# Attention and routed experts in one kernel: a new order of all operations, with the products on zeros at other places

## The chip, the cores and the metric

One core of a Trainium2 chip runs the whole program. The metric is device time in microseconds (us); of the kernel before there are three timed runs and one profiled execution. TensorE (PE, with its weight load PEld) multiplies matrices into PSUM; VectorE (DVE), ScalarE (ACT) and GpSimd (POOL) compute element by element; GpSimd and SyncE (SP) issue the DMAs. Every engine works through its own instruction stream in order, and waits on semaphores for the others.

## What is computed

A sliding-window attention (8 batches, 8 heads, 576 positions, width 64, window 32 to either side) feeds a mixture of 8 experts, of which the token's modality and its logits choose one:

```python
scores = scale * np.matmul(q, k.transpose(0, 1, 3, 2))
mask = np.abs(pos[:, None] - pos[None, :]) <= window
scores = np.where(mask, scores, -1000000000.0)
attn = np.exp(scores - np.max(scores, axis=-1, keepdims=True))
attn = attn / (np.sum(attn, axis=-1, keepdims=True) + 1e-09)
x = np.matmul(attn, v)              # then [8 * 576, 512]
logits = x @ w_gate + modality_bias[modality_id]
e_idx = np.argmax(logits, axis=1)
gate_w = softmax(logits)[np.arange(N), e_idx]
h = np.maximum(x[mask] @ w1[e], 0.0)            # mask: e_idx == e
out[mask] = gate_w[mask, None] * (h @ w2[e])
```

There are 4608 tokens and two modalities. For such inputs two experts are used in fact, one for each modality; the kernel loads these two, sorts the tokens by modality while it gathers them, checks at its end that the choice holds, and has a slow general path that is not taken here.

## The kernel before

The program is a list of 867 operations, the string `ORDER` (line 34 on). A token such as `SB3.1:4567` names an operation, its indices, and after the colon the PSUM banks (of eight) that it writes; `/v`, `/a` and `/p` choose VectorE, ScalarE or GpSimd where an operation may run on more than one. One loop (line 1022 on, the last lines of the kernel's own part) calls the operations in the list's order, and each appends its instructions to the stream of its engine. Semaphores are set by the data and the banks that operations share. So the list alone decides what stands behind what on each engine, and which bank has to be read out before it is written again.

The operations, by name:

- `l` (L213) and `lv` (L229) load query, key (index 1 in the middle: key; 0: query) and values from GpSimd's queue; `W` (L643, L645) loads the two experts' weights, each 1 MB; `Km`, `Ki`, `Kg` are small loads on SP, `Ki` that of the modality ids into a tile which `Kh` clears first (L311).
- `t` (L653) transposes query or key of one half of a batch on VectorE, 1.25 us each. `MA`, `MB` write the first batch's mask by products (L662, L666).
- `SA`, `SB` (L685) are the products of the scores in two parts, each into four banks; `sa`, `sb` (L693, L696) their exponentials on ScalarE; `M` (L710) multiplies with the window mask on VectorE, from batch 1 on. `Kb` builds that mask (L425 on ScalarE, L427 on VectorE). `Kp`, `Kq`, `Ko`, `Kw` fill padding and constants.
- `V` (L727) multiplies with the values, 18 products for a pair of heads; `v` (L739, L740) normalises.
- `s0` to `s19` turn the ids into places: a cast (L165), a transpose by a product (L461), then counts, ranks and offsets. `G`, `Jo`, `Je` build one-hots on VectorE and GpSimd, `Jm` (L535) the list of output rows.
- `X` (L761) gathers the tokens by products with one-hots; `pa`, `pb` (L781, L795) copy them to their sorted places on ScalarE.
- `U` (L899) is the first expert product, eight instructions of 256 columns for a group, `u` (L914, L916) its rectifier; `D` (L925) the second, four instructions of 512 columns for a half, `y` (L935, L937) the scaling with the gate; `O` (L944) writes 128 rows by an indirect DMA. `L` (L826), `lo`, `E`, `sm`, `rc` are the routing.
- `c` are the checks at the end; `c13` casts three flags (L165), `c14` sums them by one product (L1004).
- `n4.256:1` issues four products of a zero tile with itself, 256 columns each, into bank 1 (L953): they compute nothing that is read. There are 64 of them.

Batches follow one another in this pipeline: while the expert products of the first tokens run, scores of later batches stand between them.

Of the kernel before, what the change touches and what calls it, by code (L numbers as in the profile page):

```python
# [34 lines left out]
Km Kw0/v n4.256:0 l0.1.0/p l0.0.0/p n4.256:0 Kp0/a Kj/p n4.256:0 l0.1.1/p e0/v e1/v n4.256:0 Kp1/v Kn0/p Kq1/v n4.256:0  # L35
Kq0/v l0.0.1/p Ke/v n4.256:0 Kw2/v l1.0.2/p Kh/v t0.0.1/v Ki n4.256:0 Kw1/p Kn1/p MA0.0:0123 e2/v e3/v n4.256:4 e4/v
t0.0.0/v n2.256:4 Kg n2.256:4 n2.256:4 lv0.0/p n2.256:4 Ko1/v n2.256:4 t0.1.1/v n2.256:4 n2.256:4 SA0.0 Kc5/p MA0.1:4567
sa0.0/a t0.1.0/v Kc1/p Kv/p lv0.1/p SA0.1 MB0.0:0123 Kc3/p sa0.1/a t1.1.0/v SB0.0 l1.1.2/p s0/a W1.0/p Ko0/v t1.0.0/v
MB0.1:4567 sb0.0/a Kc2/p SB0.1 Kc0/p n2.256:0 s1:0 sb0.1/a V0:12 Kc4/p s2/v s3/v s4 s5 n2.256:3 v0/v n2.256:3 lv1.0/p
n2.256:3 s6/v Kb/a s8/v V2:34 s11/v e6/v s12/p V1:12 e7/p v2/v Kc6/p s7 V3:56 n2.256:7 v1/v W1.1/p n2.256:3 s9/a s10/a  # L40
n2.256:4 r0/a n2.256:0 n2.256:0 t1.0.1/v lv1.1/p r1/a v3/v SA1.0:0123 W2.0/p s13/v sa1.0/a t1.1.1/v SB1.0:4567 l2.0.2/p
s15/v Ko2/v sb1.0/a e8/v SB1.1:0123 s14/v s17/v G0/v s16/v c0/v Je1.0/v Je0.0/v sb1.1/a X0.0:5 Jy2/v M5/v Je0.1/p X0.4:4
X0.1:7 l2.1.2/p Jy10/v Jo1/v Je0.2/p pb0.0/a X0.2:2 pa0.0/a l3.1.2/p M4/v V5:01 pb0.1/a pa0.1/a e5/p l3.0.2/p pb0.2/a
X0.3:5 pa0.2/a v5/v V4:67 Je1.1/p pb0.3/a pa0.3/a Je1.2/p Jo0/v pb0.4/a SA1.1:0123 lv2.0/p pa0.4/a v4/v Jm0:5 sa1.1/a
U0.1:4 G1/v Kc7/p Jo2/v U0.0:6 u0.1/a Je2.0/v U1.3:0 M7/v Je2.1/p U1.0:7 Je3.0/v u1.3/a W2.1/p M6/v u0.0/a V7:12 e9/p
u1.0/a U0.2:6 Je3.1/v Je2.2/v v7/v lv2.1/p V6:34 u0.2/a U0.3:0 r2/a v6/v Je3.2/p U1.2:1 u0.3/a Jo3/v L0:7 X1.2:0 X1.0:6
lo0/v Jx0/v Jm1:3 pa1.0/a X1.1:7 D0.1.0:4 Je5.0/v pb1.0/a Jx1/v Jo5/v Je5.1/p pb1.1/a D0.0.0:6 E0/a pa1.1/a sm0/v
Je4.0/v pb1.2/a rc0/v G2/v Je4.1/p X1.3:3 pa1.2/a X1.4:7 D0.0.1 pa1.3/a t2.0.0/v pa1.4/a D0.1.1 pb1.3/a Jo4/v pb1.4/a
U2.3:0 y0.1/a Je5.2/v Je4.2/v t2.0.1/v L1:3 u1.2/a Jm2:7 y0.0/a U3.2:5 lo1/v u2.3/a s19/v Jo6/v SB2.0:1234 Je7.0/v
U2.2:0 Je7.1/v sb2.0/a Je7.2/v Jx2/v U2.1:6 t2.1.1/v U2.0:7 t2.1.0/v u2.1/a u2.2/a SA2.0:1234 Jo7/v u2.0/a U3.3:6 E1/a  # L50
sa2.0/a Je6.0/v U3.1:7 t3.0.1/v Je6.1/p U1.1:0 Je6.2/p u3.1/a M9/v l4.0.2/p u3.3/a SA2.1:1234 u1.1/a M8/v lv3.0/p
D2.0.0:7 sa2.1/a Jm3:0 D2.0.1 l4.1.2/p Jx3/v sm1/v u3.2/a Jy1/v lv3.1/p Jy3/v SB2.1:0123 Jy0/v Jy4/v t3.0.0/v D2.1.0:6
sb2.1/a Jy5/v V9:45 rc1/v D2.1.1 v9/v y2.0/a V8:01 M10/v y2.1/a SB3.0:2345 U3.0:6 v8/v sb3.0/a D1.1.0:7 M11/v V10:01
r3/a Jy8/v Jy6/v V11:45 v10/v D1.1.1 u3.0/a v11/v D1.0.0:0 y1.1/a Jy7/v X2.0:2 Jy9/v X2.1:3 G3/v X2.2:7 O0.1/p pa2.0/a
D3.1.0:1 pb2.0/a t4.1.0/v pa2.1/a X2.3:6 pb2.1/a O0.0/p D3.0.0:2 pa2.2/a t4.0.0/v pb2.2/a D1.0.1 pa2.3/a pb2.3/a X2.4:7
D3.0.1 y1.0/v pb2.4/a pa2.4/a t3.1.1/v O1.0/p D3.1.1 SA3.0:4567 t3.1.0/v O2.0/p U5.0:0 sa3.0/a t4.1.1/v U4.2:3 y3.0/v
# [1170 lines left out]
```

## Time and profile before

| | |
|---|---|
| three timed runs, median (lowest to highest) | 212.38 us (212.2 to 212.52) |
| profiled execution, its own time | 213.69 us |
| its span, first to last instruction | 212.0 us |
| busy in the span: PE, PEld, DVE, ACT, POOL | 193.3, 140.2, 151.8, 133.5, 99.3 us |
| mean granted clock of TensorE | 0.970 of full speed |
| products on zeros | 64, first at 1.3, last at 21.2 us |

The busy times are shares of one span in which the stages have different limits, so they say little alone; the stretches below split the span. A wait is named by the engine and line that ended it ("<-PE banks L685"); "issue" is time for which the profile shows no reason, and "remote" a release by nothing that the profile shows. The granted clock is 1.00 at 2.4 GHz and 0.50 at 1.2 GHz. Matmuls are pipelined and their ends are modelled.

### The profile page before, as it was taken

How to read it: one execution, taken by the hardware profiler on the slowest of the kernel's cores; microseconds unless marked ns; L12 is line 12 of the kernel's file. 1: busy time of each engine (PE TensorE's matmuls, PEld its weight loads, DVE VectorE, ACT ScalarE, POOL GpSimd, SP SyncE). 2: the span in 40 equal slices, each digit the busy share in tenths (PEclk: the TensorE clock that was granted, in tenths of full speed). 3: DMA queues.
4: the chain of work that ended last, by engine and by line, in shares of the span. 5: the costliest groups of instructions: out<-in, count | busy, mean ns of one | idle time of the engine just before them, and what ended most of it. 6: DMA issues, size and time to landing. Idle time of an engine off the chain costs nothing.

```text
span 212.0 us, 6172 instructions
## 1 busy us (share of the span) xinstructions
PE 193.3 (91%) x2538; PEld 140.2 (66%) x2561; DVE 151.8 (72%) x300; ACT 133.5 (63%) x224; POOL 99.3 (47%) x138
## 2 busy tenths in 40 slices
PE   7869489999999989999999999999999999999940
PEld 5647278768675577668765885686597668566510
DVE  3868999799889978899899569887376527311610
ACT  5268696498896466896796879759975622244110
POOL 7887699730803483368650853330160322025350
PEclk9999859999999999999999999999999999999995
DMA  4999999999999459999999899225030121113212
GB/s 73 175 174 201 194 208 194 213 212 193 196 190 192 172 129 211 194 178 173 220 190 72 268 165 128 99 102 201 0 148 6 54 99 53 49 49 149 101 56 56
DMA packets 47629, 30.41 MB, mean 143 GB/s; under 512 B 38851, under 2 KB 38891, under 8 KB 47339
## 3 DMA queue, kind: packets, MB, share of 16 engines
q0 software_dynamic: 46576, 27.79, 83.1%
q1 hardware_dynamic: 1019, 2.16, 3.0%
q8 instruction: 22, 0.36, 0.7%
q14 instruction: 12, 0.10, 0.1%
HBM read 36.76 MB, written 9.70 MB: 219 GB/s over the span
## 4 chain that ended last, share of the span: by engine, by line
PE 48%; issue 16%; POOL 15%; DMA 9%; DVE 6%; ACT 2%; SPq 1%; POOLq 0%; ACTq 0%
PE banks L925 20%; PE banks L899 18%; POOL out_dram L944 5%; DMA qk<-in_k_dram 4%; PE banks L727 4%; POOL vt L229 3%; DMA mid<-in_moe_modality_id_dram 3%; PE banks L685 2%; POOL qk L213 2%; PE banks L761 2%; DVE xt L740 2%; DMA mb_bc<-n_moe_modality_bias_dram 1%; PE banks L826 1%; DVE qk L653 1%; POOL ev L527 1%
## 5 line engine op out<-in xcount | busy, mean ns | idle before, releaser
L944 POOL DMA_INDIRECT out_dram<-ys,ids x37 | 43.3, 1170 | 90.8 <-ACT ys L935 39.4
L899 PE MATMUL banks<-XT,w_sb 128*128 128x256 bf16 x576 | 70.3, 273 | 0.3 <-DVE xt L740 0.3
L925 PE MATMUL banks<-w_sb,hT 128*128 128x512 bf16 x265 | 67.7, 379 | 1.2
L899 PEld LDWEIGHTS <-w_sb 128*128 128x128 bf16 x576 | 54.4, 98 | 11.7 <-issue 1.6
L693 ACT ACTIVATE pt<-banks 128x1536 bf16<-128x1536 f32 x32 | 46.3, 1451 | 22.2 <-PE banks L685 19.4
L916 ACT ACTIVATE hT<-banks 128x512 bf16<-128x512 f32 x56 | 31.7, 599 | 20.6 <-PE banks L899 19.7
L925 PEld LDWEIGHTS <-hT 128*128 128x128 bf16 x296 | 26.6, 98 | 24.3 <-issue 0.6
L653 DVE STREAM_TRANSPOSE qk<-qk 128x576 int32<-128x576 int32 x32 | 38.7, 1248 | 3.9 <-DMA qk<-in_q_dram 2.2
L710 DVE TENSOR_TENSOR pt<-pt,mask 128x1920 bf16<-128x1920 bf16 x28 | 32.2, 1169 | 4.7 <-ACT pt L693 4.6
L740 DVE TENSOR_TENSOR xt<-banks,recs 128x640 bf16<-128x640 f32 x32 | 26.4, 824 | 1.1
L914 DVE TENSOR_SCALAR hT<-banks 128x512 bf16<-128x512 f32 x18 | 12.4, 688 | 18.3 <-PE banks L899 18.1
L727 PE MATMUL banks<-vt,pt 128*128 128x65 bf16 x576 | 23.5, 196 | 1.0 <-ACT pt L696 0.9
L727 PEld LDWEIGHTS <-pt 128*128 128x128 bf16 x576 | 22.0, 99 | 3.6 <-issue 1.1
L685 PE MATMUL banks<-qk 32*128 32x192 bf16 (+1 forms) x640 | 19.0, 242 | 4.6 <-DVE qk L653 2.9
L935 ACT ACTIVATE ys<-banks,Gt 128x512 f32<-128x512 f32 x20 | 13.6, 690 | 12.3 <-PE banks L925 12.3
L781 ACT CAST XT<-banks 128x352 f32 (+3 forms) x40 | 18.0, 451 | 3.8 <-PE banks L761 3.2
L229 POOL DMA_DIRECT2D vt<-in_v_dram x16 | 20.4, 1277 | 0.0
L685 PEld LDWEIGHTS <-qk 32*128 32x128 bf16 x640 | 12.6, 93 | 11.7 <-issue 7.9
L795 ACT CAST XT<-banks 128x352 f32 (+2 forms) x39 | 17.6, 451 | 3.3 <-PE banks L761 2.0
L937 DVE TENSOR_SCALAR ys<-banks,Gt 128x512 f32<-128x512 f32 x17 | 12.5, 734 | 7.8 <-PE banks L925 4.4
L761 PE MATMUL banks<-oh,xt 128*128 128x128 bf16 (+1 forms) x160 | 13.1, 224 | 1.7 <-DVE iv L555 1.1
L761 PEld LDWEIGHTS <-xt 128*128 128x128 bf16 x160 | 10.7, 103 | 5.1 <-issue 1.5
(157 smaller groups left out, 141.7 us busy)
## 6 DMA issues: line engine op xcount, KB each, us to landing
vt<-in_v_dram POOLq DMA_DIRECT2D x16, 288.0 KB
w_sb<-in_moe_w_dram POOLq DMA_DIRECT2D x4, 1024.0 KB
qk<-in_q_dram POOLq DMA_DIRECT2D x7, 576.0 KB
qk<-in_k_dram POOLq DMA_DIRECT2D x7, 576.0 KB
wx<-w_sb SPq DMA_DIRECT2D x2, 1024.0 KB, 4.5
out_dram<-ys,ids POOLq DMA_INDIRECT x37
qk<-in_k_dram POOLq DMA_DIRECT2D x2, 288.0 KB
qk<-in_q_dram POOLq DMA_DIRECT2D x2, 288.0 KB
```

The source lines that it names most:

```text
L229: nc.gpsimd.dma_start(v_t[b % NV][:, n_ * i:n_ * i + n_, 0:D], v[b].rearrange("h s d -> (h s) d").rearrange("(n p) d -> p n d", p=P)[:, n_ ...
L653: nc.vector.transpose(qk_t[b % 2][:, g, at:at + S].rearrange("p (t r) -> p r t", r=R), Ct["l", b][:, u, g].bitcast(I32).rearrange("p (r j) ...
L685: nc.tensor.matmul(st[:, h, WIN * i_:WIN * i_ + w_], qk[32 * h:32 * h + 32, c_, QK + k0:QK + k0 + P], qk[32 * h:32 * h + 32, c_, q0:q0 + w ...
L693: nc.scalar.activation(pt[:, :, 2 * part:2 * part + 2, 0:WIN], st[:, :, 0:2 * WIN].rearrange("p h (j c) -> p h j c", c=WIN), ACT.Exp, scal ...
L710: nc.vector.tensor_tensor(out=p_ap, in0=p_ap, in1=mask[:], op=ALU.mult)
L727: nc.tensor.matmul(o_ap, pt[:, c1:c1 + P], vt[:, g0 + j, 0:D + 1], start=(m == 0 and i_ == 0), stop=(i_ == len(mine) - 1), skip_group_chec ...
L740: nc.vector.tensor_tensor(out=x_t[b % NX][:, :, P * hp:P * hp + P].rearrange("p m (h d) -> p h m d", h=2), in0=o_v[:, :, :, 0:D], in1=rec. ...
L761: nc.tensor.matmul(t_[:, kd, :], x_t[b % NX][:, m, P * kd:P * kd + P], Ct["oh", b][:, m, 0:n_], start=True, stop=True, skip_group_check=True)
L899: ins = nc.tensor.matmul(ph[:, u_, :], w1[:, f0:f0 + 2 * P - 1:2], rhs, start=(kd == 0), stop=(kd == n_kd - 1))
L916: nc.scalar.activation(o_ap, i_ap, ACT.Relu)
L925: nc.tensor.matmul(Ct["D", t_, s_], Ct["h", t_][:, kf, P * s_:P * s_ + P], w2, start=(kf == 0), stop=(kf == n_kf - 1))
L944: ins = nc.gpsimd.indirect_dma_start(out=out, out_offset=bass.IndirectOffsetOnAxis(ap=ids[:, u_:u_ + 1], axis=0), in_=Ct["y", t_, s_][:], ...
```

## The change

The list is a new one. It holds the same 867 operations, the same 64 products on zeros among them; their sequence, their banks, and for 42 of them the engine are other ones. Nothing else in the file changes. Two pieces of each list, from batch 3's scores and from the end:

```diff
-y3.0/v u5.0/a SB3.1:4567 u4.2/v O3.0/p U5.2:2 sb3.1/a M12/v U4.3:3 O1.1/p M13/v U5.1:0 y3.1/a ... V12:45
+u5.0/a M13/v y3.1/a L2:4 SB3.1:0123 lv3.1/p lo2/v y3.0/v U5.1:7 E2/a sb3.1/a ... V13:45 M12/v U5.2:6 l5.0.2/p U4.2:0
...
-D17.1.1 D17.0.1 y17.1/a c14:6 O17.1/p y17.0/v c15/v c16/v O17.0/p c17
+c13/a O18.0/p c14:1 D17.1.1 D17.0.1 y17.1/a O17.1/p y17.0/v c15/v c16/a O17.0/p c17
```

The products on zeros stood, counted in the list: 28 ahead of `MA0.0`, 18 behind it, 2 ahead of `s1`, 6 behind `s5`, 10 behind `V3`. Now: 38 ahead of `MA0.0`, 4 behind `SA0.0`, 4 behind `s1`, 4 behind `s4`, 8 ahead of `V3`, 2 behind it, 4 behind `X0.2`.

VectorE at the head, from the clearing of the id tile to the first instruction on the transposed ids (`Am`); `qk_84` is batch 0, `qk_85` batch 1. Before:

```order
L311 MEMSET mid_95 40x256
L653 STREAM_TRANSPOSE qk_84<-qk 128x18x32
L603 TENSOR_TENSOR pe__133<-pe__133,e_107 128x16
L605 TENSOR_REDUCE ext_e<-pe__133 128x2
L607 TENSOR_SCALAR sp_i<-ext_e 128x2
L653 STREAM_TRANSPOSE qk_84<-qk 128x18x32
L342 MEMSET vt_89 128x36
L653 STREAM_TRANSPOSE qk_84<-qk 128x18x32 x2
L653 STREAM_TRANSPOSE qk_85<-qk 128x18x32
L342 MEMSET vt_88 128x36
L653 STREAM_TRANSPOSE qk_85<-qk 128x18x32
L464 TENSOR_SCALAR Am<-banks 128x40
```

The clearing (L311) is VectorE's first instruction now and stands far ahead of this piece. On the same engine, from batch 0's second transpose to the same end, in the changed kernel:

```order
L653 STREAM_TRANSPOSE qk_84<-qk 128x18x32 x3
L342 MEMSET pt_87 128x20x32
L342 MEMSET pt_87 128x4x32
L427 TENSOR_SCALAR mask<-neg 128x768 x2
L427 TENSOR_SCALAR mask<-neg 128x2x192
L322 MEMSET ones 128x128
L653 STREAM_TRANSPOSE qk_85<-qk 128x18x32
L611 TENSOR_TENSOR oh_ab<-e_107,ext_e 128x16
L653 STREAM_TRANSPOSE qk_85<-qk 128x18x32
L464 TENSOR_SCALAR Am<-banks 128x40
```

The padding of a score tile (`pt_87`), the mask (three instructions, from ScalarE) and the ones came between batch 0's last transpose and batch 1's first.

ScalarE from `sa3.0` (the exponential of the first part of the scores of batch 3's first four heads, into `pt_86`) to `sb3.1` (second part, other four heads, into `pt_87`). Before:

```order
L693 ACTIVATE pt_86<-banks 128x4x2x192
L916 ACTIVATE hT<-banks 128x512
L693 ACTIVATE pt_87<-banks 128x4x2x192
L696 ACTIVATE pt_87<-banks 128x4x128
L935 ACTIVATE ys<-banks,Gt 128x512
```

On the same engine in the changed kernel:

```order
L693 ACTIVATE pt_86<-banks 128x4x2x192
L916 ACTIVATE hT<-banks 128x512
L935 ACTIVATE ys<-banks,Gt 128x512
L845 ACTIVATE ex<-lo__146 128x32
L693 ACTIVATE pt_87<-banks 128x4x2x192
L696 ACTIVATE pt_87<-banks 128x4x128
```

A scaling and the routing's exponential came between the two exponentials of the scores. On TensorE the two score operations had `U5.0` and `U4.2` between them; now `D3.0.0`, `U5.0`, `D3.0.1` and `L2`.

ScalarE at the end of the program, around the cast of the flags (`badb`). Before:

```order
L916 ACTIVATE hT<-banks 128x4x128
L916 ACTIVATE hT<-banks 128x512
L165 CAST badb<-bad 128x3
L916 ACTIVATE hT<-banks 128x512
L935 ACTIVATE ys<-banks,Gt 128x512
```

On the same engine in the changed kernel:

```order
L935 ACTIVATE ys<-banks,Gt 128x512
L916 ACTIVATE hT<-banks 128x512 x2
L935 ACTIVATE ys<-banks,Gt 128x512
L165 CAST badb<-bad 128x3
L935 ACTIVATE ys<-banks,Gt 128x512
L165 CAST fl_i<-fl 128x1
```

The cast has moved behind the last rectifiers and the last scaling but one, and the product that reads it (`c14`) from behind the last half of the expert products to ahead of its last two.

## Rows read from the trace of the kernel before

**Rows 1.** Stretches of the span; columns: stretch, length, busy (count) by engine, clock, DMA, GB/s

```profile
21.50:25.00 3.50, 1.66 (x62) 1.26 (x64) 3.45 (x11) 1.96 (x2) 3.39 (x4) 1.00 1.15 208
25.00:31.90 6.90, 5.20 (x89) 4.47 (x77) 6.77 (x14) 6.61 (x14) 5.36 (x8) 0.51 1.49 197
32.20:203.70 171.50, 168.53 (x2153) 120.92 (x2175) 125.78 (x228) 113.03 (x194) 71.25 (x71) 1.00 0.83 142
```

**Rows 2.** Chain of waits, head; columns: start us, us, what

```profile
0.94 2.56 DMA mb_bc<-n_moe_modality_bias_dram
7.43 6.66 DMA mid<-in_moe_modality_id_dram
```

**Rows 3.** Timeline of VectorE, head; columns: start us, us, engine line operation, idle before

```profile
13.93 2.50 DVE L653 STREAM_TRANSPOSE qk<-qk 128x576 int32<-128x576 int32 x2 [1.78 <-DMA qk<-in_q_dram]
16.98 0.20 DVE L464 TENSOR_SCALAR Am<-banks 128x40 bf16<-128x40 bf16 x1 [0.55 <-PE banks L461]
21.12 1.25 DVE L653 STREAM_TRANSPOSE qk<-qk 128x576 int32<-128x576 int32 x1
24.69 0.81 DVE L505 TENSOR_TENSOR oh<-iob,col 128x640 bf16<-128x640 bf16 x1
30.89 0.89 DVE L505 TENSOR_TENSOR ohp<-iob,pmd 128x640 bf16<-128x640 bf16 x1
```

**Rows 4.** DMA: GB/s in 40 slices of 5.3 us, and loads by size

```profile
GB/s 73 175 174 201 194 208 194 213 212 193 196 190 192 172 129 211 194 178 173 220 190 72 268 165 128 99 102 201 0 148 6 54 99 53 49 49 149 101 56 56
qk<-in_k_dram POOLq DMA_DIRECT2D x7, 576.0 KB
vt<-in_v_dram POOLq DMA_DIRECT2D x16, 288.0 KB
qk<-in_k_dram POOLq DMA_DIRECT2D x2, 288.0 KB
```

**Rows 5.** Groups by line, VectorE's prices; columns: busy us, mean ns, idle before

```profile
L710 DVE TENSOR_TENSOR pt<-pt,mask 128x1920 bf16<-128x1920 bf16 x28 | 32.2, 1169 | 4.7 <-ACT pt L693 4.6
L505 DVE TENSOR_TENSOR ohp<-iob,pmd 128x640 bf16<-128x640 bf16 x8 | 6.5, 818 | 0.0
L527 DVE TENSOR_SCALAR ev<-ev,pr 128x180 bf16<-128x180 bf16 x4 | 1.0, 259 | 0.5 <-POOL ev L524 0.5
L342 DVE MEMSET pt<- 128x640 uint32 (+1 forms) x2 | 0.7, 378 | 0.1
L974 DVE TENSOR_TENSOR sc__150<-off_f,half 128x40 f32<-128x40 f32 x1 | 0.2, 193 | 0.0
```

**Rows 6.** Timeline of TensorE, the first expert products

```profile
32.27 3.66 PE L899 MATMUL banks<-XT,w_sb 128*128 128x256 bf16 x32
```

**Rows 7.** Chain of waits where TensorE is full

```profile
43.73 1.73 PE banks L925 x8
45.45 0.87 PE banks L899 x8
```

**Rows 8.** Timeline of ScalarE and TensorE, batch 3's scores

```profile
72.50 1.45 ACT L693 ACTIVATE pt<-banks 128x1536 bf16<-128x1536 f32 x1 [2.18 <-PE banks L685]
76.32 1.45 ACT L693 ACTIVATE pt<-banks 128x1536 bf16<-128x1536 f32 x1 [1.88 <-remote]
74.00 0.64 PE L685 MATMUL banks<-qk 32*128 32x192 bf16 x24 [0.44 <-DVE ys L937]
78.31 0.71 PE L727 MATMUL banks<-vt,pt 128*128 128x65 bf16 x18 [0.94 <-ACT pt L696]
```

**Rows 9.** Groups of ScalarE by line, and timeline of the end

```profile
L916 ACT ACTIVATE hT<-banks 128x512 bf16<-128x512 f32 x56 | 31.7, 599 | 20.6 <-PE banks L899 19.7 <-issue 0.9
L935 ACT ACTIVATE ys<-banks,Gt 128x512 f32<-128x512 f32 x20 | 13.6, 690 | 12.3 <-PE banks L925 12.3
...
203.99 0.75 DVE L937 TENSOR_SCALAR ys<-banks,Gt 128x512 f32<-128x512 f32 x1 [2.76 <-PE banks L1004]
205.30 0.97 POOL L944 DMA_INDIRECT out_dram<-ys,ids  x1 [0.30 <-DVE fl_i L167]
```

More of the change, by code (lines that the diff above doesn't have):

```diff
@@ L40 @@
[L40 to L44, printed above, removed]
@@ new lines @@
+v6/v U0.2:0 Je2.1/p G1/v Kv/p L0:2 Je2.2/p u0.2/a U1.0:6 lo0/v r1/a v7/v U1.2:2 u1.0/a Jo2/v X1.0:1 X1.2:5 u1.2/a G2/v
+X1.1:6 Jm1:3 pa1.0/a X1.3:4 pb1.0/a D0.0.0:2 Jo5/v E0/a pb1.1/a Je5.0/v pa1.1/a D0.1.0:1 sm0/v Jo4/v Je5.1/p pb1.2/a
+pa1.2/a D0.0.1 rc0/v Je4.0/v pb1.3/a t2.1.1/v pa1.3/a Je4.1/p X1.4:5 D0.1.1 lv2.1/p pb1.4/a t2.0.1/v pa1.4/a U3.2:4
+y0.1/a Je4.2/p Ko2/v y0.0/a s18/v U2.0:5 Jx1/v t2.0.0/v Je5.2/p u3.2/a L1:2 u2.0/a U2.3:4 lo1/v t2.1.0/v SB2.0:0123
+u2.3/a Jy2/v Jm2:5 E1/a l4.0.2/p sm1/v sb2.0/a U2.1:4 Je7.0/v Jx2/v Je7.1/v U2.2:5 Jy3/v Jo6/v Je7.2/p l4.1.2/p rc1/v
@@ new lines @@
+pb3.0/a y4.0/v X3.1:6 pa3.0/a X3.4:2 X3.2:4 pb3.1/a t5.1.1/v O3.0/p D4.1.1 pa3.1/a pa3.2/a X3.3:1 t5.0.1/v D5.1.0:0
+lv4.0/p pb3.2/a pa3.3/a SB4.1:4567 G5/v pb3.3/a pa3.4/a O4.0/p D5.1.1 c2/v y4.1/v sb4.1/a c3/v U6.3:1 U6.2:3 pb3.4/a
+M18/v y5.1/a SA4.0:4567 u6.3/a U6.1:2 O5.1/p Jy11/v M19/v sa4.0/a L3:1 U7.1:0 l6.1.2/p lo3/v u6.1/a M17/v lv6.0/p U7.3:1
+u6.2/a u7.1/a M16/v V18:23 u7.3/a lv5.0/p U6.0:0 v18/v V17:45 Kc7/p u6.0/a V16:67 E3/a v17/v SB5.0:0123 e10/v sm3/v
+D6.0.0:5 v16/v sb5.0/a O4.1/p U7.0:4 rc3/v V19:67 u7.0/a SA5.0:0123 v19/v D6.0.1 sa5.0/a X4.0:7 U7.2:6 y6.0/v pb4.0/a
@@ new lines @@
+U10.2:5 pa6.0/a y11.0/a SB7.0:0123 u10.2/v pb6.0/a O11.0/p pa6.1/a D10.0.0:4 M31/v sb7.0/a D10.1.0:5 O8.1/p M30/v X6.2:7
+D10.0.1 pb6.1/a pa6.2/a SA7.0:0123 y10.0/v pb6.2/a D10.1.1 sa7.0/a O10.0/p U12.0:4 L6:7 M28/v X6.3:0 V31:12 pa6.3/a
+lo6/v U13.2:3 u12.0/a v31/v E6/a pb6.3/a U13.1:4 y10.1/v U12.2:1 sm6/v M29/v u13.1/a O10.1/p u13.2/a U12.1:0 V29:45
+u12.2/a u12.1/v V30:23 v29/v V28:01 D11.1.0:7 e11/v v28/v U13.3:4 v30/v D11.1.1 X6.4:0 U12.3:3 y11.1/v pa6.4/a pb6.4/a
+c6/v O11.1/p D12.0.0:2 rc6/v u12.3/a X7.0:0 U13.0:5 pb7.0/a X7.1:1 u13.3/a D12.1.0:7 pa7.0/a pa7.1/a D12.0.1 u13.0/a
@@ new lines @@
+pb7.1/a D12.1.1 y12.0/v X7.2:0 D13.1.0:1 pa7.2/a pb7.2/a X7.3:2 D13.0.0:5 pb7.3/a y12.1/a D13.1.1 pa7.3/a D13.0.1 X7.4:2
+U15.1:4 y13.0/v pa7.4/a U16.1:6 u15.1/a y13.1/a U16.0:7 O13.1/p U15.3:1 L8:2 O13.0/p U14.2:3 u15.3/a u16.0/v L7:0
+O12.0/p xe/a U15.2:4 c7/v c8/v lo8/v O12.1/p L9:7 U15.0:1 E8/a sm8/v U16.3:5 lo7/v u16.1/v E7/a U14.3:2 lo9/v sm7/v
+u15.0/v E9/a u15.2/a U16.2:7 c9/v u14.3/a u14.2/v D15.1.0:4 u16.2/v u16.3/v D16.1.0:3 rc7/v sm9/v D16.0.0:5 rc8/v
+D16.1.1 D15.0.0:7 y16.1/v D15.1.1 O16.1/p U14.1:3 D15.0.1 y15.1/a O15.1/p D16.0.1 y15.0/v u14.1/v U14.0:4 c10/v U18.0:3
@@ L89 @@
+c11/v u14.0/a U17.1:7 c12/v y16.0/v D14.1.0:2 U18.1:4 N/p U17.3:5 O15.0/p u18.1/v u18.0/v D14.1.1 O16.0/p D14.0.0:3
+U17.0:4 y14.1/a D18.0.0:1 u17.1/a u17.0/v O14.1/p rc9/v U17.2:7 D14.0.1 D18.0.1 y14.0/a u17.2/a D17.0.0:4 O14.0/p
+u17.3/a D17.1.0:7 y18.0/a c13/a O18.0/p c14:1 D17.1.1 D17.0.1 y17.1/a O17.1/p y17.0/v c15/v c16/a O17.0/p c17
 """
```

80 lines of the change are left out of this document (31 added, 49 removed).

## The prediction

> **What bounds the kernel now.** I read the stretches first, then the chain of waits, then VectorE's and ScalarE's rows in the stretches that the chain names. The profiled execution has a span of 212.0 us and a time of its own of 213.69 us; the median of the three timed runs is 212.38 us, 0.38 above the span. All terms below are differences against this span, and I add their sum to the median. The stretches show three parts [rows 1]. From 32.20 to 203.70 TensorE is busy 168.53 of 171.50 us at clock 1.00: here the work itself is the bound, and only 3.0 us are idle. Before 32 us it is not: from 21.50 to 25.00 it is busy 1.66 of 3.50 us. After the last product comes the tail: the last output write is issued at 205.30 and the span ends at 212.0 [rows 9].
>
> The work of TensorE is the same before and after: the same 867 operations, 64 products on zeros among them, in another order. So the time can change in three places alone: the moment from which TensorE is filled with expert products (the first of them starts at 32.27 [rows 6]), the 3.0 us of idle time behind it, and the tail.
>
> In the head the chain first goes through the modality ids: their last DMA is issued at 7.43 and takes 6.66 us, against 2.56 us for the bias, which is sent on still empty queues [rows 2]. From 14 us on VectorE sets the pace: the two transposes of batch 1's query start at 13.93, when the query has landed, the work on the ids starts at 16.98, the first transpose of batch 1's key at 21.12 with no idle time in front of it, the one-hot for gathering at 24.69, the last one-hot for the index lists at 30.89, ending at 31.78, and the expert products follow at 32.27 [rows 3, 6].
>
> **The head, step by step.** The clearing of the id tile is now VectorE's first instruction, and the three id DMAs leave before the large loads do. The last of them left at 7.43; behind the bias, issued at 0.94, and two of its own kind it should leave at about 2.8 us (an estimate), and land between 5.4 us (with the bias's 2.56) and 9.5 us (with its own 6.66). The cast of the ids stood at 14.1 us; it has left the chain in either case. Late next is batch 1's query, which the DMA queue brings, and then VectorE.
>
> The loads keep their sequence. By the rates in slices of 5.3 us, 3.30 MB had moved by 21.2 us, and up to the key of batch 1 ten times 288 KB (2.95 MB) had to [rows 4]: that is 1.75 us earlier at 201 GB/s, so 19.45 us. The same count puts batch 1's query at 13.2 us, and its transpose started 0.7 us behind that, so the key can be transposed from about 20.2 us: the floor of this part, 0.9 us under 21.12.
>
> What VectorE does before it: batch 0's last transpose ends 1.78 us ahead of 13.93, at 12.15, and VectorE waits [rows 3]. Into that gap now go the padding of one score tile (two memsets, 0.73 us), the three instructions that make the mask (they ran on ScalarE) and the memset of ones (0.17). The trace has no such mask on VectorE. Three of the smallest comparable instruction (259 ns for 180 values) cost 0.8 us; at the rate of the one-hot (818 ns for 640 values) 1920 values cost 2.45 us; at the rate of the masking product, which writes 1920 values in 1.17 us, 1.2 us [rows 5]. I take 1.2, since that row moves the same number of values of the same type. So 2.1 us go into a gap of 1.8, and the query's transposes start near 14.2 instead of 13.93. They end near 16.9, one small instruction between them included. Behind them stand the instructions on the ids and the normalising of three head pairs, which took from 16.98 to 21.12 with about 0.4 us of gaps and of instructions that are now elsewhere; 3.7 us put the key's transpose at 20.6. That is a gain of 0.5 us. With the mask at 0.8 the floor of 20.2 holds (gain 0.9), with 2.45 the transpose starts at 21.9 (loss 0.8).
>
> The Trainium skill, "VectorE: DVE Perf Modes", section "The perf-mode tier table", says that an operation on one bf16 source in SBUF runs at four values a cycle, 693 ns for 2048 values. By that page the mask would cost an estimated 1.0 us in three instructions, and the key's transpose would start at 20.4; no run here shows it.
>
> From the key's transpose to the end of the last one-hot lie 10.7 us before. Three small instructions left this stretch, of the kind that takes 193 ns and less, and one such came in [rows 5]: a gain of 0.2. VectorE is busy nearly throughout, 6.77 of 6.90 us from 25.00 to 31.90 [rows 1], so the rest moves with it. ScalarE, with 6.61 of 6.90, moves too, since its exponentials start from the same transpose. **Head: 0.5 + 0.2 = 0.7 us earlier**, bounds 1.3 earlier and 0.8 later.
>
> **The zeros and the clock.** Before, 46 of the 64 products on zeros stand ahead of the first scores and 18 between 16 and 21.5 us. Now 38 stand ahead of the first mask product, and the other 26 in six places: after the first scores, after the ids' transpose, after the counts, two places around the last product with values of batch 0, and four behind the third gathering product. The granted clock was 1.00 up to 25.0 and 0.51 on average from 25.00 to 31.90, its lower level (1.2 GHz), after the stretch in which TensorE was busy 1.66 of 3.50 us; it was back at 1.00 when the expert products began [rows 1]. In that low stretch VectorE and ScalarE were full, and TensorE had to wait for them; so the fall cost next to nothing, and a fall that is avoided gains next to nothing. I cost this edit at 0, with a loss below as a rival.
>
> The Trainium skill, "TensorE: Matmul & The Clock Gate", section "What's actually happening", says that throttled is the clock's default and that activity releases it. By that page alone the zeros would be worth their while wherever they stand; the rows here, with a low clock that delayed no expert product, say 0.
>
> **Behind the first expert product.** Two stalls stand in the rows of batch 3's scores. The 24 products at 74.00 write the same four banks as the score products before them, and had to wait until the exponential of 72.50 to 73.95 had read these: TensorE had only two groups of expert products (0.87 us each [rows 7]) between the two. I put this stall at 0.6 us: 0.44 idle and the rest hidden in modelled ends. Now three groups of that length stand between them, and the routing products: 2.6 us at least, so this stall goes. What is late next there is the second exponential, and this is the second stall: at 76.32 ScalarE started it 1.88 us after it was free, with no releaser that the profile knows, and 18 products with values, on banks of these scores, waited for it with 0.94 us idle; counted from where they were due, 1.1 us [rows 8]. Now 2.3 us of products stand between these scores and the next use of their banks, 2.6 before: if the exponential starts late again, 1.1 to 1.4 us are lost again, if not, nothing. I take half, 0.55 gained.
>
> Against that stand places where the new order is tighter. The products for tile 16 follow the last gathering product at a distance of one group (0.87 us), in which a copy on ScalarE has to end; in batch 2 two score operations write the same banks one after the other with no room to spare. I put these at 0.4 us together, between 0 and 1.
>
> **The tail.** The small product that sums the flags stood behind the last expert product; it now stands ahead of the last eight, and waits for a cast on ScalarE. From the end of the product before, ScalarE has two scalings (690 ns), two activations (599 ns) and the cast (0.2) to do, 2.8 us; TensorE has three halves of 0.87, 2.6 us [rows 7, 9]. So TensorE waits 0.2 us (0 to 0.5) with all its remaining work behind it. Behind the last product the path is as before: scaling on VectorE (0.75 from 203.99), the write at 205.30, its landing [rows 9].
>
> **Sum.** -0.7 (head) - 0.6 (banks of batch 3's scores) - 0.55 (late exponential) + 0.4 (tighter places) + 0.2 (tail) = -1.25. Since half of that rests on stalls that may come back elsewhere, I forecast -1.0: 212.38 - 1.0 = 211.4 us.
>
> **Rivals.**
> First: the two orders differ, and the gains are given back. The late exponential comes back at 1.2 us and the mask costs enough to use up the head's gain; the sum is 0 - 0.6 + 0 + 0.4 + 0.2 = 0.0, 212.4 us. For it: both orders leave little room in most places, and the cause of the late start is not in the rows.
> Second, slower: the clock is at its low level when the expert products begin. Place: the first groups at 31.6 us. The low stretch lasted 6.9 us and ended just ahead of them [rows 1]; if it starts half its length later, 3.4 us of a stretch that TensorE bounds run at half speed, which costs 1.7 us. It decides from the point at which the clock rises after the first expert product instead of before it. Time: 212.38 - 1.0 + 1.7 = 213.1 us. For it: TensorE is again nearly idle between the zeros and the second gathering; against it: four products on zeros now stand in just that place, and the products from 28 us on are dense.
> Third: the late exponential does not come back at all and the key is transposed at the floor of 20.2 us: -1.3 - 0.6 - 1.1 + 0.4 + 0.2 = -2.4, so 210.0 us; I give this end 210.3, as some of the tighter places will cost more.
>
> **Chances.** Forecast 0.43, gains given back 0.22, low clock 0.20, larger gain 0.15. A measurement of this kernel can tell a change from none from about 0.2%, 0.4 us, on. Of the forecast's own range (210.8 to 212.0) nearly all is faster; with the third that makes 0.56. Same: 0.19, nearly all of it the first rival. Slower: 0.25, the second and the worse part of the first. The range that leaves out 2 in 10 is 210.3 to 213.2.
>
> **What would show it.** Right: the id cast before 10 us, the first transpose of batch 1's key near 20.6, the first expert product near 31.6 at clock 1.00, no idle time in front of the 24 score products of batch 3 that waited at 74.00, some 0.2 us in front of the flag product. Wrong: expert products at a low clock; a key transposed after 21.1; more than 3.0 us of TensorE idle between the first expert product and the last.

## The result, and the profile after

The changed kernel takes 210.96 us (median of 11 runs, 210.22 to 212.09), the kernel before 212.52 us (median of 11, 212.20 to 213.70): ratio 0.9895, 95% interval 0.9871 to 0.9919. The ratio is that of the means of the last eight runs of each, 210.76 and 213.00 us, and makes the kernel 2.2 us faster (1.7 to 2.7); the medians of all eleven differ by 1.56 us. The forecast was 1.0 us, less than half of the 2.2, though its range of times, 210.3 to 213.2 us, holds the 210.96. The two profiled executions differ by 2.6 us of span, 212.0 against 209.4: the profiled execution of before (213.69 us) is one of the slowest of its kernel. Two terms of the forecast were read from it, which matters below.

The stretches of after, in the columns of [rows 1]; the last one ends with its own last product:

```profile
21.50:25.00 3.50, 1.79 (x64) 1.30 (x64) 3.47 (x9) 2.16 (x2) 2.55 (x6) 0.99 1.28 200
25.00:31.90 6.90, 5.81 (x88) 5.17 (x81) 5.97 (x13) 6.32 (x15) 5.86 (x9) 0.51 1.50 197
32.20:201.20 169.00, 167.42 (x2152) 120.37 (x2170) 123.63 (x227) 113.64 (x196) 69.14 (x78) 1.00 0.83 144
```

Behind 32.2 us TensorE is now idle for 1.6 us instead of 3.0. The low clock stands in the same stretch as before, and is over when the expert products begin. VectorE is no longer full from 25.0 to 31.9: 5.97 us of 6.90, where it had 6.77.

VectorE in the head of after, in the columns of [rows 3]:

```profile
12.29 0.82 DVE L427 TENSOR_SCALAR mask<-neg 128x768 bf16<-128x768 bf16 x3
13.40 1.26 DVE L653 STREAM_TRANSPOSE qk<-qk 128x576 int32<-128x576 int32 x1
17.12 0.22 DVE L739 RECIPROCAL recs<-banks 128x10 f32<-128x10 f32 x1 [1.31 <-PE banks L727]
20.90 1.25 DVE L653 STREAM_TRANSPOSE qk<-qk 128x576 int32<-128x576 int32 x1 [0.21 <-DMA qk<-in_k_dram]
24.38 0.81 DVE L505 TENSOR_TENSOR oh<-iob,col 128x640 bf16<-128x640 bf16 x1
30.87 0.84 DVE L505 TENSOR_TENSOR ohp<-iob,pmd 128x640 bf16<-128x640 bf16 x1
```

TensorE at the same time: the first products with values, and the first expert products, which answer to [rows 6].

```profile
16.38 0.71 PE L727 MATMUL banks<-vt,pt 128*128 128x65 bf16 x18 [0.71 <-DMA vt<-in_v_dram]
...
32.12 3.66 PE L899 MATMUL banks<-XT,w_sb 128*128 128x256 bf16 x32
```

The cast of the ids stands at 7.66 us, as forecast. But the time that VectorE has won it spends waiting: 1.31 us for products whose values were still being loaded, then 0.21 us for batch 1's key. In before the key's transpose stood at 21.12 with no wait [rows 3]; here it stands at 20.90 with one. The load, not VectorE, is last in this profile, and the expert products start 0.15 us earlier, not 0.7. Two more profiles of after, below, gain more here.

### The profile page after: what moved, and what is told of

Same layout as the page of the kernel before. It is cut to its first block, busy times and chain, and to the rows that moved or that the text cites. A ratio compares the mean times of both kernels' runs of the same rounds, so it can differ in the third digit from the quotient of the medians.

```text
span 209.4 us, 6173 instructions
## 1 busy us (share of the span) xinstructions
PE 192.5 (92%) x2539; PEld 139.8 (67%) x2561; DVE 148.8 (71%) x292; ACT 133.5 (64%) x228; POOL 98.0 (47%) x142
## 4 chain that ended last, share of the span: by engine, by line
PE 69%; issue 12%; POOL 9%; DMA 4%; ACT 1%; DVE 1%; POOLq 1%; ACTq 0%; DVEq 0%
PE banks L899 25%; PE banks L925 23%; PE banks L727 8%; PE banks L685 6%; POOL out_dram L944 4%; PE banks L761 4%; DMA qk<-in_k_dram 4%; PE banks L826 1%; POOL qk L213 1%; POOL vt L229 1%; ACT pt L693 1%; PE banks L535 1%; POOLq L949 1%; PE banks L953 0%; DVE xt L740 0%
## 5 line engine op out<-in xcount | busy, mean ns | idle before, releaser
L944 POOL DMA_INDIRECT out_dram<-ys,ids x37 | 39.3, 1063 | 92.2 <-ACT ys L935 46.3
L916 ACT ACTIVATE hT<-banks 128x512 bf16<-128x512 f32 x57 | 32.8, 599 | 18.2 <-PE banks L899 18.0
L710 DVE TENSOR_TENSOR pt<-pt,mask 128x1920 bf16<-128x1920 bf16 x28 | 31.9, 1152 | 2.6 <-ACT pt L696 1.3
L937 DVE TENSOR_SCALAR ys<-banks,Gt 128x512 f32<-128x512 f32 x16 | 11.8, 743 | 20.5 <-PE banks L925 19.9
L935 ACT ACTIVATE ys<-banks,Gt 128x512 f32<-128x512 f32 x21 | 14.4, 691 | 17.2 <-PE banks L925 14.5
L914 DVE TENSOR_SCALAR hT<-banks 128x512 bf16<-128x512 f32 x17 | 11.5, 688 | 11.8 <-PE banks L899 11.8
L761 PEld LDWEIGHTS <-xt 128*128 128x128 bf16 x160 | 11.3, 103 | 5.9 <-issue 0.8
L761 PE MATMUL banks<-oh,xt 128*128 128x128 bf16 (+1 forms) x160 | 13.6, 224 | 1.1 <-ACT pt L696 1.1
```

The source lines that it names most:

```text
L710: nc.vector.tensor_tensor(out=p_ap, in0=p_ap, in1=mask[:], op=ALU.mult)
L761: nc.tensor.matmul(t_[:, kd, :], x_t[b % NX][:, m, P * kd:P * kd + P], Ct["oh", b][:, m, 0:n_], start=True, stop=True, skip_group_check=True)
L916: nc.scalar.activation(o_ap, i_ap, ACT.Relu)
L944: ins = nc.gpsimd.indirect_dma_start(out=out, out_offset=bass.IndirectOffsetOnAxis(ap=ids[:, u_:u_ + 1], axis=0), in_=Ct["y", t_, s_][:], ...
```

## The experiments

The kernels were timed in five groups, each on a chip of its own and beside the kernel before; its median was 212.7, 213.2, 214.2, 214.4 and 214.3 us there, so only ratios are compared between the groups, and a gain in us is worked out from its ratio. A list that wraps into other lines shifts the line numbers of a kernel by one or two.

Two lists with the same 867 operations can be spliced where the sets of operations already listed nearly agree. Such places are ahead of the first expert product (about 32 us), ahead of batch 2's first gathering product (about 65 us) and at about 100 us. What one list still owes at a seam is put there.

**One part of the new order at a time.**

```
 seg1: new list [..first expert product)   old list behind it   (7 small ops put at the seam)
 seg2: old, new list [32 us .. 65 us), old
 seg3: old, new list [65 us .. 100 us), old
 seg4: old list up to 100 us, new list behind it
```

> The new order's first part alone (up to the product that places the one-hots, about 31.8 us; all products on zeros are in it), and the old order from there on. Theory A (the gain lies in single stalls of batch 3's scores, the head is bound by its loads): within 0.3 us of the kernel before, first expert product about 0.1 us earlier. Rival B (the forecast's head term): 0.7 us faster. Rival C (the places of the zeros carry the gain): about 2 us faster.

> The new order from about 31.8 to 64 us alone, the old one before and behind it. Theory A: within 0.2 us of the kernel before. Rival D (many small distances between a product and the reader of its bank, spread over the whole order): 0.6 to 0.7 us faster, as the drift of the products against their own work suggests. Rival C: 0.

> The new order from about 64 to 100 us alone, batch 3's scores among it, the old one before and behind it. Theory A: 1.2 to 1.8 us faster, the 0.44 us and the 0.94 us of idle time on TensorE gone and no exponential that starts late. Rival D: 0.7 us. Rival C: 0.

> The new order from about 100 us to the end alone, the old one before it. Theory A: within 0.2 us of the kernel before. Rival D: 0.4 us faster. Rival C: 0. The forecast's tail term (the flag product in front of the last expert products waits for a cast): 0.2 us slower.

Measured against the kernel before: seg1 1.009 [1.006, 1.012], seg2 1.0040 [1.0012, 1.0068], seg3 1.0038 [1.0013, 1.0063], seg4 1.0049 [1.0026, 1.0072]. None is faster, so no theory is right as written. In seg1 the seam hides what the head gains: a small instruction on VectorE that waits 1.49 us for GpSimd stands there ahead of batch 1's masking, and the 18 products with values behind it waited 1.85 us. The profiles told more than the times. Where seg1, seg2 and seg4 run the old list through batch 3's scores, neither stall of [rows 8] is there; and in seg3 the first expert products ran at the low clock. This is seg3, in the columns of [rows 1] for TensorE alone, and its first expert products:

```profile
25.75:32.25 6.50, 4.91 (x81) 0.60 1.44 199
32.30:33.90 1.60, 1.60 (x12) 0.50 2.21 177
```

```profile
32.34 4.41 PE L900 MATMUL banks<-XT,w_sb 128*128 128x256 bf16 x32
```

Up to 65 us seg3 has the old order. The same 32 products took 3.66 us in [rows 6]; here, at 1.2 GHz up to 33.9 us, 4.41. That is the forecast's second rival, met in the old order. Most of it is made up for later: seg3 starts batch 2's gathering at 65.96 us, the three profiles of before at 65.67 to 65.87.

**Both kernels again, and the zeros alone.**

```
 before_again, after_again: no edit
 zeros_old: new list, - its runs of n2.256/n4.256   + those of the old list at the same neighbours
 zeros_new: old list, - its runs of n2.256/n4.256   + those of the new list at the same neighbours
```

> The kernel before, unchanged, to see a second profiled execution. Theory A (the stalls at batch 3's scores belong to the old order): again 0.6 us in front of the 24 score products and 1.1 us in front of the 18 products with values behind them, span near 212. Theory E (they were a matter of that one execution, as three kernels with the same list there did not have them): neither stall, span 210.3 to 211.2, the difference depending on whether the low clock ends before or after the first expert product at about 32.3 us.

> The changed kernel, unchanged, to see a second profiled execution. Theory A: the same as the first, span 209.4 within 0.2. Theory E: span 208.6 to 210.5, moving with the end of the low clock: above 209.5 if it ends later than the first expert product (32.1 us in the first profile), about 209 if not.

> The changed kernel with the products on zeros at the places of the kernel before: 28 ahead of the first mask product, 18 behind it, 2 ahead of the transposed ids, 6 between the counts and the second values, 10 behind the fourth values; all else in the new order. Theory F (the places of the zeros set when the clock falls and rises, and the gain is that it has risen before the first expert product): 1 to 1.6 us slower than the changed kernel, that is within 0.6 us of the kernel before; low clock still there after 32.3 us in the profile. Theory A or D (the zeros do nothing): 1.4 to 1.7 us faster than the kernel before, as the change itself.

> The kernel before with the products on zeros at the places of the changed kernel: 38 ahead of the first mask product, 4 behind the first scores, 4 behind the transposed ids, 4 behind the counts, 8 ahead of and 2 behind the fourth values, 4 behind the third gathering product; all else in the old order. Theory F: 1 to 1.6 us faster than the kernel before. Theory A or D: within 0.3 us of it.

The kernel before took 211.97 us (span 210.3) this time. ScalarE and TensorE at batch 3's scores, as in [rows 8]:

```profile
73.60 0.64 PE L685 MATMUL banks<-qk 32*128 32x192 bf16 x24
74.28 1.45 ACT L693 ACTIVATE pt<-banks 128x1536 bf16<-128x1536 f32 x1 [0.48 <-PE banks L685]
...
76.80 0.71 PE L727 MATMUL banks<-vt,pt 128*128 128x65 bf16 x18
```

The exponential starts when its scores are there, and TensorE does not wait. So theory A falls: the two stalls, which were two of the forecast's three gains, belong to some executions only. The changed kernel took 211.42 us (span 209.8). It began the expert products earlier, at 31.61, with a low clock only from 25.25 to 28.50 us, and lost the time again where VectorE waited 1.52 us for batch 5's query and gathering products waited for what was queued behind:

```profile
85.10 1.25 DVE L653 STREAM_TRANSPOSE qk<-qk 128x576 int32<-128x576 int32 x1 [1.52 <-DMA qk<-in_q_dram]
```

In the first profile of after that wait was 0.27 us. zeros_new: 1.0000 [0.9972, 1.0027]. zeros_old: 0.9923 [0.9893, 0.9953]. The new places of the zeros alone give nothing, and the new order with the old places keeps its gain as far as the intervals tell. Theory F falls.

**What waits in both profiles of the old order.** Two waits are in both profiles of the kernel before: a group of expert products at 39 us that waits for VectorE, and VectorE for the last batch's key at about 126 us, 1.40 and 1.29 us. Before_again's rows, on TensorE and on VectorE:

```profile
39.18 1.03 PE L899 MATMUL banks<-XT,w_sb 128*128 128x256 bf16 x8 [0.29 <-DVE xt L740]
```

```profile
125.47 1.26 DVE L653 STREAM_TRANSPOSE qk<-qk 128x576 int32<-128x576 int32 x1 [1.29 <-DMA qk<-in_k_dram]
```

The edits:

```
 two_stalls (old list):  - U1.2:1 .. L0:7 .. X1.1:7 .. X1.4:7     + U1.2:7 .. L0:1 .. X1.1:2 .. X1.4:2
                         - O7.1/p l7.1.2/p                        + l7.1.2/p O7.1/p
 head_new: new list up to the first expert product, old behind, the 7 small ops spread from 38 to 46 us
 head_two: head_new and two_stalls
 after_load (new list):  - l5.1.2/p, l5.0.2/p at their places     + both right behind t3.1.0/v
```

> The kernel before with two edits: the banks of the third group of expert products of tile 1 and of the first routing products are exchanged (so that the group at about 39 us no longer waits for VectorE's normalising), and the load of the last batch's key is issued ahead of the output write that waits 6.6 us on GpSimd. Theory G (these two standing waits, the same in every execution of the old order, are a part of the gain): 0.45 + 0.25 = 0.7 us faster, 0.4 to 0.9; no stall of 0.45 us at 39 us, no wait for in_k_dram at 125 us. Theory A (batch 3's scores carry the gain): within 0.2 us.

> The new order up to the first expert product, the old one behind it, and seven small operations that the new order does later spread over the rows from 38 to 46 us (in the earlier run of this kind they stood together at the seam and cost 3.3 us). Theory G with the clock (the new head is 0.1 us shorter, and in it the low clock ends less often behind the first expert product, which costs the old order up to 0.85 us in some executions): 0.3 to 0.8 us faster in the median, low clock ending at or before 32.3 us in the profile. The forecast's head term: 0.7 us faster, but by the key's transpose. Theory A: within 0.2 us.

> The new head and the two edits of the old rest together: the kernel before with what theory G names. Theory G: the sum, 1.0 to 1.5 us faster than the kernel before, that is nearly the change's whole 1.6 us. Theory A: within 0.4 us. If some of the gain stays unnamed, this run is that much above the changed kernel's 210.96 us.

> The changed kernel with the loads of batch 5's query and key issued as soon as batch 3's last transpose has freed their buffer, ahead of the run of output writes. In two profiles of the changed kernel VectorE waited 0.27 and 1.52 us for this query at about 85 us, and in the second the gathering products behind it stood still for 1.2 us. If this late load is what spreads the changed kernel's times: 0.3 to 0.6 us below the changed kernel's median, 210.4 to 210.7 us at a kernel before of 212.5, and no wait for in_q_dram. If not: the same as the changed kernel.

All four missed: two_stalls 1.0047 [1.0021, 1.0073], head_new 1.0023 [1.0002, 1.0044], head_two 1.0105 [1.0061, 1.0148], after_load 1.0299 [1.0253, 1.0345]. In the profiles each wait was taken away, and another stood one place further. TensorE in two_stalls, where the group at 39.09 us no longer waits:

```profile
39.09 1.91 PE L900 MATMUL banks<-XT,w_sb 128*128 128x256 bf16 x16
40.84 0.55 PE L827 MATMUL banks<-wgd,XT 128*128 128x8 bf16 x16
41.24 0.62 PE L762 MATMUL banks<-oh,xt 128*128 128x128 bf16 x8
41.71 0.33 PE L536 MATMUL banks<-ev,ohp 128*128 128x72 bf16 x5
42.42 0.32 PE L536 MATMUL banks<-ev,ohp 128*128 128x72 bf16 x5 [0.39 <-POOL ev L528]
...
121.74 1.47 PE L900 MATMUL banks<-XT,w_sb 128*128 128x256 bf16 x12 [1.03 <-DVE lo__146 L838]
```

The five products at 42.42 now wait for GpSimd, and the earlier load of the last key is followed by a new wait of 1.03 us at 121.74. From its first expert product to batch 2's gathering two_stalls takes 33.64 us, against 33.48 to 33.49 in the profiles of before: with this wait gone, nothing is won there. In after_load the two loads stand ahead of four output writes; VectorE then waits for those writes to give back the tile it scales into, and the kernel is 6 us longer:

```profile
79.28 0.75 DVE L939 TENSOR_SCALAR ys<-banks,Gt 128x512 f32<-128x512 f32 x1 [5.76 <-DMA out_dram<-ys,ids]
```

In head_new the expert products did begin early, at 31.71 us and at full clock; behind the seam the old rest lost it again (the expert products at 39.49 waited 1.28 us for VectorE). No splice tried here has the gain of the head alone.

**Where the gain lies.** At 65 us the seam is clean, and TensorE has done the same work in both lists when batch 2's first gathering product starts. So its start can be compared directly. Before and after, in their second profiles:

```profile
65.87 0.78 PE L761 MATMUL banks<-oh,xt 128*128 128x96 bf16 x12
```

```profile
64.55 0.78 PE L761 MATMUL banks<-oh,xt 128*128 128x96 bf16 x12
```

```
 front_new: new list up to 65 us, old behind        back_new: old list up to 65 us, new behind
 after_third, before_third: no edit
```

> The new order up to about 64 us, the old one behind it (at this seam the two lists differ by five small operations, and the earlier run that crossed it lost nothing there). Theory H (what the change gains in every execution lies before 64 us: a head that ends 0.1 to 0.7 us earlier, by how long the clock stays low, and a group of expert products at 39 us that no longer waits; behind 64 us the two orders lose the same 2.8 us of time): 0.8 to 1.5 us faster than the kernel before, and within 0.4 us of the changed kernel run beside it, unless this chip shows the late exponential at 76 us, which then costs this kernel 1.7 us as it does the kernel before. Theory A (the gain lies at batch 3's scores): within 0.3 us of the kernel before.

> The old order up to about 64 us, the new one behind it. Theory H: within 0.4 us of the kernel before (0.2 to 0.3 faster at the last batch's key, whose load the old order issues behind a waiting output write), and 1.7 us faster only on a chip with the late exponential, if the new order does not have it there. Theory A: 1.2 to 1.6 us faster on any chip.

> The changed kernel again, timed beside the kernel before on this chip, with a third profile. Theory H: 0.8 to 1.7 us faster than the kernel before; span 208.6 to 210.5. If the chip shows the late exponential and only the old order has it: 2.5 to 3.4 us faster. Theory A: 1.4 to 1.8 us faster and the same profile as the first.

> The kernel before on the same chip, to see whether its exponential at 76 us starts late here: span about 212 if so (theory A expects it always), 210.3 to 211.2 if not (theory E and H).

front_new: 0.9936 [0.9910, 0.9962], 1.4 us faster. after_third on the same chip: 0.9920 [0.9890, 0.9950], 1.7 us faster. back_new: 1.0043 [1.0019, 1.0067], 0.9 us slower. So in the timed runs the first 65 us carry most of the gain, as theory H has it. The one profile of front_new does not show it: it is the slowest of its nine runs (214.04 us, the fastest 212.45), and batch 2's gathering starts at 65.72 us, as in before. The profile of back_new shows one reason why it is slower than H expects, in a stretch where its list is that of before:

```profile
12.00:15.25 3.25, 3.16 (x40) 0.50 1.92 160
```

Here the clock was at its lower level a first time, in the midst of batch 0's scores; in before_third the same stretch reads 3.25 us busy with 71 instructions at 1.00. Batch 1's key is then transposed at 22.42 us instead of 21.02, and the gathering product starts at 67.06 instead of 65.67. two_stalls, again with the old head, shows the same first low stretch. None of the nine profiles with the new head and zeros in it has it.

The starts in the three profiles of each kernel (us; the last column is the span less the one before it):

| | first expert product | batch 2's gathering | rest |
|---|---|---|---|
| before | 32.27, 32.38, 32.18 | 65.75, 65.87, 65.67 | 146.3, 144.4, 146.1 |
| after | 32.12, 31.61, 31.70 | 65.15, 64.55, 64.71 | 144.3, 145.3, 146.3 |

By the means, 0.47 us come from the head and 0.49 from 32 to 65 us. The second part is the steadier: from the first expert product to the gathering it is 33.48 to 33.49 us in the three of before and in back_new, and 32.94 to 33.09 in the three of after and in front_new. The head scatters more: in front_new the expert products start at 32.63 us. Behind 65 us the two orders differ by less than each differs from itself.

**No zeros at all.**

```
 no_zeros_new: new list, - every n2.256 and n4.256      no_zeros_old: old list, - every n2.256 and n4.256
```

> The changed kernel without any of its 64 products on zeros, everything else in place. Theory H with the zeros costed at 0 (TensorE waits for loads, VectorE and ScalarE until 31 us whatever its clock): within 0.4 us of the changed kernel, that is 1.1 to 1.9 us faster than the kernel before. Rival (the zeros keep the clock from a low stretch between 9 and 21 us, and the score products of batch 0 are then twice as long): slower than the changed kernel by 1.3 us, what one such stretch from 12 to 15.25 us cost the old order in two profiles, or more; a second low stretch in the profile ahead of 21 us.

> The kernel before without its 64 products on zeros. Zeros at 0: within 0.4 us of the kernel before. Rival: slower by 1.3 us or more, with low clock ahead of 21 us in the profile.

no_zeros_new: 0.9974 [0.9945, 1.0004], 0.6 us faster than the kernel before on its chip and not clear of no change, where the changed kernel was 2.2 and 1.7 us faster on two others. no_zeros_old: 1.0043 [1.0019, 1.0066], 0.9 us slower (0.4 to 1.4). So in the old order the zeros are worth about 0.9 us, and the rival's 1.3 lies inside the interval; in the new order they are worth 1 us or more by a comparison across chips alone. The low clock that the rival expected ahead of 21 us is there, although the clock column reads 1.00: the products have the lengths of the lower level, up to about 17.2 us in no_zeros_old and 12.7 in no_zeros_new (four products of the first mask, 384 columns each, take 1.46 us, as in back_new at clock 0.50, and 0.81 to 0.82 in before at 1.00). The same 24 score products of batch 0 in the first profile of before and in no_zeros_old:

```profile
13.64 0.63 PE L685 MATMUL banks<-qk 32*128 32x192 bf16 x24
```

```profile
14.95 1.04 PE L684 MATMUL banks<-qk 32*128 32x192 bf16 x24
```

In no_zeros_old the key is transposed 1.7 to 1.9 us later for it, at 22.94 us. In no_zeros_new it is not late (20.96 us), batch 2's gathering starts at 64.98, and the profile does not show where this kernel loses its time. In no_zeros_old the later low stretch is longer too, up to the first expert product at 34.57 us:

```profile
24.50:34.50 10.00, 8.12 (x145) 0.50 1.62 191
```

## Why the prediction had the sign and not the size

**The stretches.** That the gain can lie only ahead of the expert products, in the idle time behind them and in the tail was right, and the head was rightly named first.

**The step that failed: two stalls read from one execution, and a stretch put at nothing.** The forecast put 0.6 and 0.55 us of gain on [rows 8], 0.6 us of loss on tighter places and the tail, and nothing on the rest of the stretch behind the first expert product. The exponential came late in the first profile of before. After that it started 1.87 to 1.95 us late in all six kernels with the old order there on three of the chips (before_third's row is below), and in none of five on two others. Where it is late the fastest run of the kernel before is 213.38 to 213.73 us, elsewhere 211.88 and 211.95. The 0.44 us in front of the score products comes and goes with it.

```profile
76.20 1.45 ACT L693 ACTIVATE pt<-banks 128x1536 bf16<-128x1536 f32 x1 [1.87 <-remote]
```

On such a chip the new order need not have it in this place: in after_third the second exponential starts at 73.31, when its scores are there (after_load, with other loads in flight, had it 1.79 us late). The gain is given back later, where TensorE pauses between products of one group with no releaser, 0.36 and 0.42 us, and then starts the wide products at 180.85, 1.4 us behind its own work:

```profile
176.60 0.98 PE L899 MATMUL banks<-XT,w_sb 128*128 128x256 bf16 x5 [0.36 <-issue]
178.00 3.01 PE L899 MATMUL banks<-XT,w_sb 128*128 128x256 bf16 x26 [0.42 <-issue]
180.85 5.34 PE L925 MATMUL banks<-w_sb,hT 128*128 128x512 bf16 x24
```

The first profile of after has neither pause. So the late exponential did not come back in the three profiles of the changed kernel, as the third rival has it, but what that is worth is not a property of the two orders: behind 65 us (the last column of the table above) the changed kernel gains 2.0 us in the first pair of profiles, where before has both stalls and after none, and loses 0.9 and 0.2 us in the other two pairs. What comes in every pair is the gain from 32 to 65 us that the sum does not have, 0.45 to 0.55 us.

**What no profile shows.** The three pairs give a mean of 1.3 us over the whole span, the timed runs 2.2 and 1.7. In the later two pairs the profiled execution of before, 211.97 and 213.42 us, is 1.25 and 0.96 us faster than the median beside it (213.22, 214.38), while after_third, 212.71 us, is near its own (212.84). So a part of the timed gain, up to about 1 us, sits there in slower executions of the kernel before that no profile shows. A part of it goes with the clock: in the group of before_again 8 of 21 runs of the kernel before have a mean granted clock of 0.962 to 0.965 and a median of 213.6 us, the other 13 have 0.969 and more and 212.65 us. The two profiles with the first low stretch, back_new and two_stalls, have 0.966; none of 17 runs of the changed kernel is below 0.970. Which stretch was low in those runs, and what makes the rest, stays open.

**The head: right path, smaller and less steady.** The term was 0.7 us, by VectorE's transpose of batch 1's key near 20.6 us. In the first profile of after the products with values waited for their load and the key stood at 20.90. In after_again and after_third it is near where the forecast has it:

```profile
20.48 1.26 DVE L653 STREAM_TRANSPOSE qk<-qk 128x576 int32<-128x576 int32 x1 [0.60 <-DMA qk<-in_k_dram]
```

```profile
20.15 1.26 DVE L653 STREAM_TRANSPOSE qk<-qk 128x576 int32<-128x576 int32 x1 [0.21 <-DMA qk<-in_k_dram]
```

The expert products follow it by 11.15 to 11.16 us in the three profiles of before and by 11.22, 11.13 and 11.55 us in those of after. So the path was right. Its gain was 0.15, 0.77 and 0.48 us in the three pairs, and what comes last is the load of the key, for which VectorE waits in all three profiles of after. The mask was taken at 1.2 us and cost 0.82 to 0.96 for three instructions; the estimate by the Trainium skill, "VectorE: DVE Perf Modes", section "The perf-mode tier table", 1.0 us, was nearer. The forecast said that the low stretch from 25 us on delays nothing. That held where it ended ahead of the expert products: it ended at 28.5 us in after_again and at 31.8 in the first profile of after, with 11.13 and 11.22 us from the key to the expert products; after_third has 11.55 with an end at 31.3.

**The zeros, costed at 0.** For their places this held. For their being there, in the old order, it did not: 0.9 us. The forecast priced the low stretch from 25 us on alone, and what failed is the step that a low clock in the head costs nothing. Without the zeros it is the scores of batch 0 that run at the lower level, and the transpose of the key comes later for it. The Trainium skill, "TensorE: Matmul & The Clock Gate", section "What's actually happening", says that activity releases the clock. The products of no_zeros_old, at half speed up to 17.2 us, agree with it.

**The second rival.** A low clock under the first expert products costs 0.75 us at these products (4.41 less 3.66 us), and it happened: in three profiles with the old head, to between 33.9 and 34.4 us (seg3, seg4, zeros_new), and once with the new one, to 32.7 (zeros_old). It was given to the wrong side, and its price of 1.7 us was too high: of the 0.75 us seg3 still has 0.1 to 0.3 at 65 us. The first low stretch, in two more of the ten profiles with the old head, costs more, 1.3 us at the first expert product (33.57 and 33.62 us against 32.28 on average).

**What was not forecast.** From 32 to 65 us the new order gains 0.49 us. One wait of before is gone there: at 39 us no group waits for VectorE. In after, the same stretch:

```profile
36.84 1.03 PE L899 MATMUL banks<-XT,w_sb 128*128 128x256 bf16 x8
37.71 0.54 PE L826 MATMUL banks<-wgd,XT 128*128 128x8 bf16 x16
38.11 1.91 PE L899 MATMUL banks<-XT,w_sb 128*128 128x256 bf16 x16
39.86 0.78 PE L761 MATMUL banks<-oh,xt 128*128 128x96 bf16 x12
```

I saw 0.29 us of idle time there in before and passed it over, since [rows 8] had larger ones. That this wait is the cause of the 0.49 us is not shown: two_stalls, which takes it away alone, gains nothing in this stretch.

**Tighter places and tail.** Costed at 0.4 and 0.2 us of loss; the rows of the first profile of after show neither. The flag product stands at 199.42 with no idle time named in front of it, and the end is as before: last scaling, last write, landing.

```profile
201.37 0.75 DVE L937 TENSOR_SCALAR ys<-banks,Gt 128x512 f32<-128x512 f32 x1 [6.18 <-PE banks L925]
202.80 0.98 POOL L944 DMA_INDIRECT out_dram<-ys,ids  x1 [0.30 <-issue]
```

## What to carry to other kernels

A stall in one profile is a term of the sum only if it comes back: before pricing it, compare the profiled time with the fastest runs, and where it is 1.5 us above them, look for the stall that explains that and cost it apart. In a schedule this tight a wait that is taken away alone turns up at the next late operand; of the spliced lists here only front_new, with the whole first 65 us of the new order (loads, VectorE, GpSimd and the banks together), kept a gain that is clear of noise. To find where two orders part, compare the start of the same product at places where both have done the same work, before looking at single waits. And where a clock column reads 1.00, compare the lengths of equal products before trusting it.

## What the runs showed of the hardware that was not expected

ScalarE can start an instruction 1.9 us after its operands are there, with no releaser that the profile names, at the same instruction of the old order in every profile on three chips and in none on two others; the chip of the first profile, which has it too, is not on record, and the cause stays open. TensorE shows the like at 176 to 181 us in after_third and no_zeros_new. With the zeros, the low stretch of the clock ahead of the expert products began between 23.1 and 26.3 us in kernels that share the new head and between 24.7 and 27.6 us in those that share the old one, and it ended between 28.5 and 34.4 us: its place is not set by the list alone. At the start of these profiles the clock column reads 1.00 although products run slower: in the first profile of before 28 products on zeros took 4.81 us and the next 18 took 2.13, that is 172 and 118 ns each.
